# A fused attention and two-layer kernel on one core: layer two of batch 3 in seven half-size products, and a new order of all pieces

## The chip, the core and the metric

The kernel runs on one core of one Trainium2 chip. A core has five engines that run side by side and wait for each other by semaphores: TensorE (PE, matrix products; its weight loads are a row of their own, PEld), VectorE (DVE), ScalarE (ACT), GpSimd (POOL) and SyncE (SP, which issues transfers). SBUF is the core's working memory, PSUM the small memory that PE writes its products to, in banks; POOL does not read PSUM. The metric is the device time of one execution in microseconds (us), less being better; each time given is the median of a few runs.

## What is computed

The input is x (8 batches, 8 heads, 512 tokens, 64 features) and state (8, 8, 32, 64). Tokens read the state and the state reads the tokens, each with a softmax; both results go, with the heads side by side (512 features), through a layer of 2048 and back:

```python
scores = scale * np.matmul(x, state.transpose(0, 1, 3, 2))
a = softmax(scores)                      # over the 32 states
xread = np.matmul(a, state)
a2 = softmax(scores transposed)          # over the 512 tokens
sread = np.matmul(a2, x)
x = concatenate([xread, sread], axis=2)  # 544 rows a batch, heads joined: 4352 x 512
h = x @ w_in                             # 512 -> 2048
g = s * relu(h) ** 2 + b
out = g @ w_out                          # 2048 -> 512
```

Inputs and output are 32-bit floats; the kernel computes its products in 16-bit floats and adds up in 32 bits.

## The kernel before, in words

The kernel is a set of small pieces and one long list of words, ORDER (line 15). A loop at the end (line 720) walks the list and calls one function a word: the word's first part is the piece, the rest its arguments (V, A and G mean VectorE, ScalarE and GpSimd; numbers are batch, block, half). No scheduler moves anything afterwards: each engine executes its own instructions in the order in which the list issues them, and waits where a semaphore is not yet up. The order of the list is therefore the schedule.

A batch passes through these pieces:

- x.b (line 176) issues two transfers of the batch's tokens on GpSimd's queue; for batch 0, four transfers on SyncE bring 32-bit tokens (xf), which castx turns to 16 bits. xT transposes on DVE. T.b (line 290) is 16 packed products that give the scores. U, mu, D, E1, z, At and A are the token softmax: transpose, maximum, difference, exponential on ACT, sum and reciprocal, product, transpose back. keep copies the scores to SBUF.
- M.b.j (line 422) is 8 packed products, state times a quarter j of w_in, so that layer one takes the softmax weights A instead of xread; Mc copies it to SBUF. "Packed" means that several small products use parts of PE's array at once.
- l.b.f (line 474) is layer one for 128 of the 2048 hidden features: two products of 512 columns, and a relu on ACT. lh.b.f.p does two such f for half of the tokens (batch 0). s and sh square the result on the engine named, into the batch's tile g.
- nm, nms, E2, a2, aps, a2T, V and srd are the other softmax, over tokens, and the state's read; V is 32 packed products a batch.

Layer two comes in two forms. The plain form is L.b.rr.q (line 497): four products of 512 columns for 128 tokens, 16 pieces and 64 products a batch, and out.b.rr (lines 509 and 517) scales by s, adds the bias and stores. The other form splits the batch's g and w_out into 2 x 2 blocks and needs seven block products instead of eight, at the price of sums. P.b.u (line 582) is half of one block product: 8 products of 256 columns, 14 pieces and 112 products a batch. S.b.i (line 561) makes the sums of blocks of g; sum 1, 2 and 4 are written over blocks of g, sum 3 into a tile of its own, and sum 3 has to read block (1, 0) before sum 1 writes it. wsum (line 528) makes the sums T1 to T4 of w_out's blocks once. ev.b.name (line 596) takes a product out of PSUM, scaled, added to the bias or to what is there; there are seven a batch, and put (line 604) issues two stores each on SyncE. Before the change, batches 0 to 3 use the plain form and batches 4 to 7 the seven products. The state rows of all batches (lsr, ssr, S_sr, P_sr, ev_sr) go through the same two layers at the end, also with seven products.

```python
    PRODUCTS = [
        ("X", (0, 0), (0, 0)), ("Y", (0, 1), (1, 0)), ("X", (0, 0), "T2"), ("W", (1, 0), "T1"),
        ("X", None, "T3"), ("W", (0, 1), (1, 1)), ("X", (1, 1), "T4"),
    ]
```

X, Y and W are PSUM banks; X is written four times on top of itself and taken out after each, W twice.

idle.n (line 663) is n products of ones by ones that nobody reads.

Buffers set further waits. Layer one has two PSUM banks (ps_h), layer two and the idle products two (ps_o), and an argument of T and M chooses one of two double banks (ps_t, ps_a). GpSimd's transfers go round eight semaphores: the ninth is issued when the first has landed. The words win.j and wout.q load quarters of w_in (two transfers) and w_out (one), st the states of the later batches.

Of the kernel before, what the change touches and what calls it, by code (L numbers as in the profile page):

```python
# [12 lines left out]


ORDER = [
    "win.0 castx.0.0.V castx.1.0.A idle.2 idle.5 idle.9 casts.V xT.0.0.0 pair.0.4 xT.0.1.0 T.0.1.0 U.0.0 "
    "sb mu.0.0 win.1 castx.1.1.A xT.0.1.1 x.1 D.0.V.0 E1.0.0 castx.0.1.V xT.0.0.1 turn.0.4.A z.0.0 "
    "At.0.V.0 A.0.0 M.0.0.0 Mc.0.0.A keep.0.0 win.2 T.0.0.1 U.0.1 M.0.1.1 Mc.0.1.A mu.0.1 D.0.V.1 "
    "keep.0.1 E1.0.1 xT.1.0 lh.0.2.0 M.1.0.0 Mc.1.0.A lh.0.0.0 xT.1.1 T.1.1 lh.0.6.0 wout.0 z.0.1 "
    "At.0.V.1 A.0.1 lh.0.2.1 win.3 U.1 M.0.2.0 lh.0.0.1 Mc.0.2.V wout.1 sh.0.2.1.V keep.1 sh.0.0.0.G mu.1 "  # L20
    "sh.0.2.0.G lh.0.4.0 wout.2 sh.0.4.0.G D.1.V L.0.0.0 l.0.11 M.1.1.0 Mc.1.1.A L.0.1.0 l.0.8 sh.0.6.0.V "
    "l.0.9 M.0.3.0 Mc.0.3.V M.1.2.1 x.2 l.0.10 Mc.1.2.V wout.3 E1.1 z.1 lh.0.6.1 At.1.V s.0.8.2.A L.0.0.1 "
    "l.0.13 L.0.1.1 l.0.14 cps.0 cps.1 cps.2 M.1.3.1 A.1 Mc.1.3.V l.0.12 s.0.12.2.V s.0.10.2.G l.0.15 "
    "s.0.14.2.A L.0.1.2 l.1.4 l.1.7 L.0.0.2 l.1.1 l.1.2 sh.0.6.1.V st xT.2 x.3 pair.4.16 cps.3 L.0.0.3 "
# [12 lines left out]
    "l.3.0 L.2.0.1 M.4.1.1 Mc.4.1.A M.4.2.0 l.3.3 L.2.0.2 l.3.1 l.3.5 s.2.12.4.V s.3.0.4.A aps.4 xT.5 "
    "L.2.1.3 Mc.4.2.V l.3.6 l.3.8 wsum.T1.0.V L.2.0.3 L.3.0.0 l.3.14 turn.12.16.A l.3.15 T.5.1 out.2.1 "
    "l.3.4 s.3.4.2.A a2T.4.V out.2.0 L.2.2.0 L.2.2.1 L.2.2.2 L.2.2.3 nm.5 V.4 U.5 nms.5.A mu.5 D.5.G "
    "wsum.T1.1.V E2.5.1 E2.5.0 M.4.3.1 srd.4 l.3.12 out.2.2 x.6 A.4 l.3.9 xn.5 a2.5 nm.2 nms.2.V xn.2 "  # L40
    "s.3.6.2.A L.2.3.0 l.3.13 E2.2.1 Mc.4.3.A wsum.T2.2.V aps.5 a2T.5.V l.3.10 L.2.3.1 L.2.3.2 L.2.3.3 "
    "l.3.11 V.3 E1.5 l.4.2 l.4.14 L.3.2.0 L.3.2.1 srd.3 out.2.3 l.4.13 M.5.1.0 Mc.5.1.A M.5.0.1 l.4.3 "
    "Mc.5.0.A s.3.8.4.V L.3.2.2 s.3.12.4.V l.4.6 xT.6 x.7",
    "l.4.0 L.3.0.1 l.4.1 s.4.0.2.A z.5 L.3.2.3 T.6.1 U.6 M.5.2.0 E2.2.0 l.4.15 l.4.5 L.3.0.2 L.3.0.3 "
    "s.4.2.2.A wsum.T3.1.G l.4.9 nm.6 L.3.1.0 Mc.5.2.A l.4.4 L.3.1.1 out.3.2 out.3.0 l.4.12 At.5.G A.5 "
    "wsum.T3.0.G a2.2 nm.0 L.3.1.2 nms.6.A L.3.1.3 l.4.7 s.4.12.2.V s.4.14.2.V E2.6.0 aps.2 a2T.2.V "
    "out.3.1 l.4.11 L.3.3.0 E2.6.1 mu.6 l.4.8 s.4.4.4.V L.3.3.1 L.3.3.2 xT.7 l.4.10",
    "l.5.0 s.4.10.2.V V.5.2 srd.5 L.3.3.3 out.3.3 srd.2 l.5.1 M.5.3.0 M.6.0.1 s.4.8.2.V Mc.5.3.A D.6.G "
    "a2.6 E1.6 P.4.0 l.5.3 P.4.1 Mc.6.0.A ev.4.X1 l.5.7 l.5.13 P.4.2 P.4.3 M.6.2.0 S.4.3.2.V S.4.1.0.V "
    "S.4.1.1.V M.6.1.1 nms.0.A E2.0.1 S.4.2.0.V S.4.2.1.V l.5.2 Mc.6.2.A l.5.6 S.4.4.2.G ev.4.Y P.4.4 "  # L50
    "Mc.6.1.A P.4.5 z.6 l.5.4 ev.4.X2 s.5.0.2.A aps.6 a2T.6.V P.4.6 l.5.12 P.4.7 T.7.1 s.5.12.2.A keep.7 "
    "s.5.2.2.A At.6.V A.6 l.5.10 ev.4.W1 P.4.8 P.4.9 l.5.14 nm.7 wsum.T4.2.V ev.4.X3 P.4.10 P.4.11 "
    "ev.4.W2 E2.0.0 nms.7.A l.5.8 a2.0 l.5.5 s.5.4.4.V xn.6 xn.0 P.4.12 aps.0 l.5.15 s.5.14.2.G U.7 mu.7 "
    "a2T.0.A P.4.13 ev.4.X4 l.5.9 l.6.3 put.4.0.0 P.5.0 l.6.2 l.5.11 D.7.G V.6.0 s.5.8.2.V srd.6 l.6.9 "
    "l.6.8 srd.0 s.5.10.2.V E1.7 S.5.3.0.V S.5.3.1.V P.5.2 P.5.1 l.6.5 ev.5.X1 P.5.3",
    "l.6.0 l.6.1 M.6.3.0 S.5.1.2.V Mc.6.3.A xn.7 xn.1 M.7.0.1 Mc.7.0.A l.6.7 ev.5.Y P.5.6 P.5.7 z.7 "
    "S.5.2.2.V M.7.1.1 Mc.7.1.A E2.7.1 l.6.15 s.6.0.4.V l.6.14 nm.1 S.5.4.1.G P.5.4 P.5.5 ev.5.X2 ev.5.W1 "
    "l.6.10 M.7.2.1 S.5.4.0.V E2.7.0 M.7.3.0 Mc.7.3.A At.7.V P.5.8 l.6.13 l.6.4 P.5.9 a2.7 l.6.11 "
    "s.6.8.2.A s.6.4.2.G P.5.10 ev.5.X3 P.5.12 s.6.10.2.A l.6.6 A.7 l.7.2 nms.1.A E2.1.1 P.5.11 l.6.12 "
    "P.5.13 aps.7 l.7.3 ev.5.W2 Mc.7.2.V l.7.10 s.6.6.2.G E2.1.0 P.6.2 a2T.7.A l.7.6 s.6.14.2.V ev.5.X4 "  # L60
    "s.6.12.2.V S.6.3.0.V S.6.3.1.V a2.1 P.6.0 P.6.1 ev.6.X1 l.7.7 l.7.8 S.6.1.2.V put.4.0.1 S.6.2.0.V "
    "S.6.4.0.G S.6.2.1.V P.6.3 l.7.11 l.7.1 aps.1 P.6.4 P.6.5 a2T.1.A put.4.1.0 put.4.1.1 l.7.5 l.7.4 V.1",
    "l.7.0 ev.6.Y P.6.6 P.6.7 s.7.0.2.A s.7.2.2.A srd.1 ev.6.X2 P.6.8 P.6.9 l.7.14 ev.6.W1 P.6.10 l.7.9 "
    "put.5.0.0 ev.6.X3 put.5.0.1 l.7.13 V.7 srd.7 l.7.15 s.7.8.2.V s.7.10.2.V s.7.14.2.V l.7.12 P.6.12 "
    "P.6.13 ev.6.X4 s.7.12.2.V lsr.13 lsr.12 S.6.4.1.G P.6.11 ev.6.W2 lsr.7 s.7.4.4.G S.7.3.0.G lsr.14 "
    "P.7.0 P.7.1 S.7.3.1.G S.7.1.1.V lsr.4 lsr.2 P.7.2 S.7.1.0.G ssr.12.2.A ev.7.X1 S.7.2.1.V lsr.15 "
    "lsr.6 P.7.3 put.5.1.0 lsr.10 lsr.11 S.7.2.0.V ev.7.Y P.7.4 S.7.4.0.V P.7.6 P.7.5 ssr.14.2.V lsr.1 "
    "ev.7.X2 ssr.6.2.V lsr.3 P.7.7 ev.7.W1 lsr.5 ssr.4.2.V",
    "lsr.0 ssr.0.2.V P.7.8 P.7.9 ssr.2.2.V S_sr.3.0.V ev.7.X3 lsr.9 S.7.4.1.V lsr.8 P.7.10 P.7.11 "
    "ssr.8.2.A ssr.10.2.V S_sr.3.1.G put.5.1.1 put.6.0.0 S_sr.1.2.V S_sr.2.2.G S_sr.4.0.G put.6.0.1 "  # L70
    "put.6.1.0 put.6.1.1 ev.7.W2 P.7.12 put.7.0.0 put.7.0.1 P.7.13 ev.7.X4 P_sr.0 put.7.1.0 "
    "ev_sr.0.0.X.0.0 P_sr.1 ev_sr.0.0.Y.1.1 P_sr.2 P_sr.3 put.7.1.1 S_sr.4.1.G ev_sr.0.1.X.0.0 P_sr.4 "
    "ev_sr.1.1.W.0.0 P_sr.5 ev_sr.1.1.X.1.1 P_sr.6 ev_sr.0.1.W.1.1 ev_sr.1.0.X.0.1",
]


# [677 lines left out]
```

## Time and profile before

| what | us |
|---|---|
| median of 3 runs | 223.57 (223.21 to 225.01) |
| the profiled execution | 222.87 |
| its span, first to last instruction | 221.1 |
| TensorE's mean granted clock in it | 0.977 |

The profile is one execution. Its page gives the busy time of each engine, then the span in 40 slices of 5.5 us with the busy share in tenths and, as PEclk, the clock that TensorE was granted. The largest groups on PE and on the other engines (columns: line, engine, operation, output and inputs, count, then busy us and mean ns of one, then idle time of the engine just before them and what ended it):

```
L461 ACT ACTIVATE r<-hps 128x512 f16<-128x512 f32 x120 | 68.1, 600 | 23.4 <-PE hps L457 23.1
L457 PE MATMUL hps<-A,M 128*128 128x512 f16 x240 | 65.8, 380 | 0.0
L501 PE MATMUL ops<-w_out,g 128*128 128x512 f16 x256 | 62.1, 379 | 0.0
L136 PEld LDWEIGHTS <-g 128*128 128x128 f16 x384 | 37.3, 98 | 9.7 <-DVE g L571 0.8
L467 POOL TENSOR_TENSOR g<-r 128x1024 f16<-128x1024 f16 (+1 forms) x9 | 18.8, 2101 | 14.9 <-ACT r L461 14.9
L571 POOL TENSOR_TENSOR g<-g 128x1024 f16<-128x1024 f16 (+1 forms) x5 | 13.6, 2731 | 18.6 <-DVE g L571 18.6
L571 DVE TENSOR_TENSOR g<-g 128x1024 f16<-128x1024 f16 (+1 forms) x15 | 13.3, 915 | 1.2 <-POOL S L571 1.1
L511 DVE SCALAR_TENSOR_TENSOR osb<-ops,sb_bc,bias_bc 128x512 f32<-128x512 f32 x16 | 11.7, 737 | 4.3 <-PE ops L501 4.2
L600 DVE SCALAR_TENSOR_TENSOR osx<-opf_X,sb_bc,bias_bc 128x512 f32<-128x512 f32 x12 | 8.9, 741 | 7.1 <-PE opf_X L136 6.3
```

hps is layer one's PSUM tile, ops layer two's in the plain form, opf_X, opf_Y and opf_W the banks of the seven products; rows of the helper mm stand as L136. The mean of a PE row is longer than the distance between two starts, since products are pipelined. A mean that mixes forms says so.

### The profile page before, as it was taken

Reading aid. Unit: us, or ns where it says so; the run is one execution under the profiler, and the core shown is the slowest. Engines: PE = TensorE matmul, PEld = TensorE weight load, DVE = VectorE, ACT = ScalarE, POOL = GpSimd, SP = SyncE. Lnnn points to the kernel's source line nnn. Section 1 sums busy time; section 2 is a strip of 40 time slices with the busy share of each in tenths; the row PEclk is TensorE's granted clock in tenths of the full one; section 3 lists DMA queues with packets and bytes.
Section 4 is the critical chain, followed back from the end, with each engine's and each line's share of the span. In section 5 each row is a group of like instructions: output and inputs, shape, how many; then the busy total and the mean of one; then the engine's idle time right before and its main releaser. Section 6 shows DMA issues by size and latency. Waiting matters only on the chain.

```text
span 221.1 us, 4579 instructions
## 1 busy us (share of the span) xinstructions
PE 209.8 (95%) x1859; PEld 120.5 (54%) x1859; DVE 172.6 (78%) x235; ACT 152.8 (69%) x258; POOL 99.9 (45%) x100
## 2 busy tenths in 40 slices
PE   7359999999999999999999999999999999999993
PEld 2124434443444435454344567777567777888882
DVE  2698998889788995697486979999985943776952
ACT  3266985988876789788886698968888767542300
POOL 8235554175057031085850507839336089250280
PEclk9955999999999999999999999999999999999999
DMA  6999997419749620449933220896900800071065
GB/s 161 224 207 206 204 165 84 86 65 134 115 69 177 128 47 0 98 80 139 220 62 76 47 52 0 99 189 114 172 6 5 185 3 0 3 166 26 3 149 135
DMA packets 23416, 22.67 MB, mean 103 GB/s; under 512 B 4196, under 2 KB 16996, under 8 KB 23396
## 3 DMA queue, kind: packets, MB, share of 16 engines
q0 software_dynamic: 16560, 12.26, 38.8%
q1 hardware_dynamic: 6160, 9.97, 18.4%
q8 instruction: 14, 0.23, 0.4%
q10 hardware_dynamic: 676, 0.16, 0.3%
q14 instruction: 6, 0.05, 0.1%
HBM read 25.72 MB, written 8.91 MB: 157 GB/s over the span
## 4 chain that ended last, share of the span: by engine, by line
PE 87%; DMA 4%; DVE 4%; ACT 1%; SPq 1%; issue 1%; DVEq 0%
PE ops L501 25%; PE hps L457 24%; PE opf_X L136 12%; PE opf_W L136 6%; PE mps L136 4%; DMA xf<-in_x_dram 3%; PE opf_Y L136 2%; PE vps L136 2%; PE aps L136 2%; PE ops_sr_X L136 2%; PE hps_sr L457 2%; PE T_None L136 2%; PE hph L136 1%; DMA out_dram<-osx 1%; PE ops_sr_W L136 1%; SPq L608 1%
## 5 line engine op out<-in xcount | busy, mean ns | idle before, releaser
L461 ACT ACTIVATE r<-hps 128x512 f16<-128x512 f32 x120 | 68.1, 600 | 23.4 <-PE hps L457 23.1
L457 PE MATMUL hps<-A,M 128*128 128x512 f16 x240 | 65.8, 380 | 0.0
L501 PE MATMUL ops<-w_out,g 128*128 128x512 f16 x256 | 62.1, 379 | 0.0
L136 PEld LDWEIGHTS <-g 128*128 128x128 f16 x384 | 37.3, 98 | 9.7 <-DVE g L571 0.8
L501 PEld LDWEIGHTS <-g 128*128 128x128 f16 x256 | 24.6, 98 | 29.3 <-issue 0.6
L457 PEld LDWEIGHTS <-M 128*128 128x128 f16 x240 | 21.5, 98 | 23.4 <-issue 5.8
L467 POOL TENSOR_TENSOR g<-r 128x1024 f16<-128x1024 f16 (+1 forms) x9 | 18.8, 2101 | 14.9 <-ACT r L461 14.9
L151 ACT CAST M<-mps 128x1024 f16<-128x1024 f32 x23 | 23.1, 1014 | 2.5 <-PE mps L136 2.5
L467 DVE TENSOR_TENSOR g<-r 128x1024 f16<-128x1024 f16 (+1 forms) x22 | 20.5, 945 | 2.7 <-ACT r L461 2.6
L571 POOL TENSOR_TENSOR g<-g 128x1024 f16<-128x1024 f16 (+1 forms) x5 | 13.6, 2731 | 18.6 <-DVE g L571 18.6
L465 ACT ACTIVATE g<-r 128x1024 f16<-128x1024 f16 (+1 forms) x19 | 21.6, 1148 | 0.2
L191 POOL DMA_DIRECT2D xn<-in_x_dram x32 | 18.6, 596 | 2.8 <-PE vps L136 2.4
L321 POOL TENSOR_TENSOR Dm<-U,mu 128x1024 f32<-128x1024 f32 x3 | 7.0, 2343 | 20.4 <-DVE mu L317 20.3
L136 PE MATMUL opf_X<-w_T,g 128*128 128x256 f16 x128 | 15.8, 273 | 0.2 <-DVE g L571 0.2
L136 PE MATMUL mps<-w_in,stT 64*32 64x512 f16 x256 | 11.8, 410 | 3.9 <-ACT stT L151 3.3
L511 DVE SCALAR_TENSOR_TENSOR osb<-ops,sb_bc,bias_bc 128x512 f32<-128x512 f32 x16 | 11.7, 737 | 4.3 <-PE ops L501 4.2
L600 DVE SCALAR_TENSOR_TENSOR osx<-opf_X,sb_bc,bias_bc 128x512 f32<-128x512 f32 x12 | 8.9, 741 | 7.1 <-PE opf_X L136 6.3
L461 ACT ACTIVATE r_sr<-hps_sr 128x256 f16<-128x256 f32 x16 | 6.0, 384 | 11.9 <-PE hps_sr L457 8.4
L571 DVE TENSOR_TENSOR g<-g 128x1024 f16<-128x1024 f16 (+1 forms) x15 | 13.3, 915 | 1.2 <-POOL S L571 1.1
L313 DVE STREAM_TRANSPOSE U<-T_None 128x1024 f32<-128x1024 f32 x7 | 8.7, 1238 | 4.6 <-PE T_None L136 3.7
L629 POOL TENSOR_TENSOR g_sr<-g_sr 128x512 f16<-128x512 f16 (+1 forms) x4 | 6.0, 1521 | 12.6 <-ACT g_sr L465 12.5
L151 DVE CAST M<-mps 128x1024 f16<-128x1024 f32 x9 | 10.8, 1208 | 0.8 <-PE mps L136 0.8
(101 smaller groups left out, 316.8 us busy)
## 6 DMA issues: line engine op xcount, KB each, us to landing
xn<-in_x_dram POOLq DMA_DIRECT2D x32, 128.0 KB, 6.4
out_dram<-osx SPq DMA_DIRECT2D x32, 128.0 KB, 2.4
xh<-in_x_dram POOLq DMA_DIRECT2D x14, 256.0 KB, 6.0
out_dram<-osb SPq DMA_DIRECT2D x24, 128.0 KB, 3.8
w_in<-in_moe_w_in_dram POOLq DMA_DIRECT2D x8, 256.0 KB, 10.4
w_out<-in_moe_w_out_dram POOLq DMA_DIRECT2D x4, 512.0 KB, 10.0
xf<-in_x_dram SPq DMA_DIRECT2D x4, 256.0 KB, 7.8
out_dram<-osb SPq DMA_DIRECT2D x4, 256.0 KB
```

The lines of the kernel that those rows point to most:

```text
L136: return nc.tensor.matmul(out, lhsT, rhs, start=start, stop=stop, tile_position=tp, is_transpose=is_transpose, skip_group_check=skip,)
L151: (engine.copy if engine is nc.scalar else engine.tensor_copy)(out, in_)
L191: nc.gpsimd.dma_start(out=xn_t[b][32 * jh : 32 * jh + 32].rearrange("t h c d -> t h (c d)"), in_=x[b].rearrange("h (t jh c) d -> jh t h (c ...
L313: nc.vector.transpose(part(U, p), part(at[b]["T", p], p))
L457: nc.tensor.matmul(hps, lhsT, rhs, start=(i == 0), stop=(i == len(terms) - 1))
L461: nc.scalar.activation(R_t[tag, q][:, i], hps, AF.Relu)
L465: nc.scalar.activation(g, r, AF.Square)
L467: e.tensor_mul(g, r, r)
L501: nc.tensor.matmul(ops_t[tag, rr], G_t[tag][:, f, P * rr : P * rr + P], w_out_f(f), start=(f == 0), stop=(f == NKF - 1),)
L511: nc.vector.scalar_tensor_tensor(osb, ops_t.pop((tag, rr)), s_bc, bias_bc, ALU.mult, ALU.add)
L571: e.tensor_tensor(out, x, y, op)
L600: nc.vector.scalar_tensor_tensor(out, fast(b, name[0]), s_bc, out if plus else bias, ALU.mult, ALU.add)
```

## The change

Only the list ORDER differs; no function does. It does four things:

- Batch 3 goes over to the seven products: its 16 L and four out are gone, 14 P, seven ev, six S and four put are there. Since the sums of w_out are needed by then, they are made earlier, and some on another engine (T1 on GpSimd, T3 on VectorE, T4 half and half).
- The unread products of the head are 10, 8 and 4 (in three places: at the start, behind sb, and behind T.0.0.1) instead of 2, 5 and 9 (all at the start): 22 instead of 16.
- Every other piece is still there, but in a new order, and some squares and copies are on another engine.
- In GpSimd's queue of transfers the order becomes win.0, x.1, win.1, wout.0, win.2, win.3 and, behind the first two squares, wout.1, wout.2, wout.3, x.2, st; before it was win.0, win.1, x.1, win.2, wout.0, win.3, wout.1 and then, with squares between, wout.2, x.2, wout.3, st.

The head, one stretch around batch 3's products, and the end (all other lines of the list are replaced in the same way; line numbers behind the list grow by one):

```diff
 ORDER = [
-    "win.0 castx.0.0.V castx.1.0.A idle.2 idle.5 idle.9 casts.V xT.0.0.0 pair.0.4 xT.0.1.0 T.0.1.0 U.0.0 "
-    "sb mu.0.0 win.1 castx.1.1.A xT.0.1.1 x.1 D.0.V.0 E1.0.0 castx.0.1.V xT.0.0.1 turn.0.4.A z.0.0 "
-    "At.0.V.0 A.0.0 M.0.0.0 Mc.0.0.A keep.0.0 win.2 T.0.0.1 U.0.1 M.0.1.1 Mc.0.1.A mu.0.1 D.0.V.1 "
-    "keep.0.1 E1.0.1 xT.1.0 lh.0.2.0 M.1.0.0 Mc.1.0.A lh.0.0.0 xT.1.1 T.1.1 lh.0.6.0 wout.0 z.0.1 "
-    "At.0.V.1 A.0.1 lh.0.2.1 win.3 U.1 M.0.2.0 lh.0.0.1 Mc.0.2.V wout.1 sh.0.2.1.V keep.1 sh.0.0.0.G mu.1 "
-    "sh.0.2.0.G lh.0.4.0 wout.2 sh.0.4.0.G D.1.V L.0.0.0 l.0.11 M.1.1.0 Mc.1.1.A L.0.1.0 l.0.8 sh.0.6.0.V "
...
-    "l.4.0 L.3.0.1 l.4.1 s.4.0.2.A z.5 L.3.2.3 T.6.1 U.6 M.5.2.0 E2.2.0 l.4.15 l.4.5 L.3.0.2 L.3.0.3 "
...
-    "lsr.0 ssr.0.2.V P.7.8 P.7.9 ssr.2.2.V S_sr.3.0.V ev.7.X3 lsr.9 S.7.4.1.V lsr.8 P.7.10 P.7.11 "
-    "ssr.8.2.A ssr.10.2.V S_sr.3.1.G put.5.1.1 put.6.0.0 S_sr.1.2.V S_sr.2.2.G S_sr.4.0.G put.6.0.1 "
-    "put.6.1.0 put.6.1.1 ev.7.W2 P.7.12 put.7.0.0 put.7.0.1 P.7.13 ev.7.X4 P_sr.0 put.7.1.0 "
-    "ev_sr.0.0.X.0.0 P_sr.1 ev_sr.0.0.Y.1.1 P_sr.2 P_sr.3 put.7.1.1 S_sr.4.1.G ev_sr.0.1.X.0.0 P_sr.4 "
-    "ev_sr.1.1.W.0.0 P_sr.5 ev_sr.1.1.X.1.1 P_sr.6 ev_sr.0.1.W.1.1 ev_sr.1.0.X.0.1",
+    "castx.1.0.V win.0 casts.V idle.10 turn.0.4.A pair.0.4 castx.0.0.V xT.0.0.0 xT.0.1.0 T.0.1.0 U.0.0 "
+    "mu.0.0 castx.1.1.A keep.0.0 sb idle.8 D.0.V.0 xT.0.1.1 castx.0.1.V E1.0.0 x.1 z.0.0 xT.0.0.1 "
+    "At.0.V.0 M.1.0.0 Mc.1.0.A M.0.0.1 A.0.0 Mc.0.0.A win.1 T.0.0.1 U.0.1 mu.0.1 D.0.V.1 keep.0.1 idle.4 "
+    "lh.0.0.0 wout.0 lh.0.2.0 xT.1.0 M.0.1.0 xT.1.1 E1.0.1 z.0.1 T.1.1 Mc.0.1.A lh.0.4.0 win.2 win.3 "
+    "sh.0.0.0.G At.0.V.1 A.0.1 keep.1 sh.0.2.0.G sh.0.4.0.V lh.0.6.0 L.0.1.0 U.1 lh.0.4.1 lh.0.0.1 wout.1 "
+    "sh.0.6.0.V sh.0.4.1.V mu.1 D.1.V lh.0.2.1 M.0.2.1 Mc.0.2.A lh.0.6.1 sh.0.6.1.V wout.2 L.0.0.0 l.0.8 "
...
+    "L.2.3.2 l.3.14 s.3.12.4.A l.3.4 L.2.3.3 out.2.3 M.5.0.1 Mc.5.0.A V.4 srd.4 a2.5 s.3.8.4.V L.2.2.0 "
+    "At.4.G L.2.2.1 L.2.2.2 A.4 l.4.2 l.4.6 L.2.2.3 M.5.2.1 E1.5 s.3.4.4.V S.3.3.2.V S.3.1.0.G M.4.3.0",
+    "l.4.0 Mc.4.3.A xT.6 P.3.0 S.3.2.0.G l.4.1 out.2.2 l.4.3 nms.2.A z.5 P.3.1 ev.3.X1 l.4.9 E2.2.1 "
+    "S.3.1.1.V S.3.2.1.G aps.5 Mc.5.2.V E2.2.0 a2T.5.V l.4.11 a2.2 P.3.4 l.4.5 P.3.2 P.3.3 S.3.4.2.V "
...
+    "lsr.13 P.7.6 P.7.7 ssr.4.2.A ev.7.W1 P.7.8 ssr.6.2.V S.7.4.0.V S_sr.1.0.V lsr.10 lsr.15 P.7.9 lsr.11 "
+    "P.7.10 ev.7.X3 lsr.14 ssr.14.2.V lsr.12 ssr.12.2.V ssr.10.2.V S_sr.3.1.V S_sr.2.0.V S_sr.3.0.G "
+    "S_sr.1.1.V S_sr.2.1.V P.7.11 ev.7.W2 P.7.12 P.7.13 P_sr.0 P_sr.1 ev_sr.0.0.X.0.0 put.7.0.0 ev.7.X4 "
+    "ev_sr.0.0.Y.1.1 P_sr.2 ev_sr.0.1.X.0.0 S_sr.4.2.V put.7.0.1 put.7.1.0 put.7.1.1 P_sr.3 P_sr.4 "
+    "ev_sr.1.1.W.0.0 P_sr.5 ev_sr.1.1.X.1.1 ev_sr.0.1.W.1.1 P_sr.6 ev_sr.1.0.X.0.1",
 ]
```

90 rows, old and new, of the table ORDER are left out of this document.

## The prediction, made before the changed kernel was run

> **What bounds the kernel now.** I read the page's busy shares and slices, then the chain of waits, then the head in windows, then the timeline where the chain leaves TensorE.
>
> ```profile
> PE 209.8 (95%) x1859; PEld 120.5 (54%) x1859; DVE 172.6 (78%) x235; ACT 152.8 (69%) x258; POOL 99.9 (45%) x100
> PE   7359999999999999999999999999999999999993
> PEclk9955999999999999999999999999999999999999
> ```
>
> TensorE (PE) is full from slice 5 (22 us) to the end; only the head has gaps, and there the granted clock is half. A busy PE need not be at its pace, so the chain of waits (start, length, what) is read for the pace:
>
> ```profile
> 44.88 1.73 PE ops L501 x8
> 46.61 0.86 PE hps L457 x4
> 47.47 0.56 PE mps L136 x16
> 48.02 0.54 PE hps L457 x2
> ...
> 139.66 1.75 PE opf_X L136 x16
> ```
>
> A 512-column product takes 1.73/8 = 216 ns, a 256-column one of the half-size kind 1.75/16 = 109 ns. These are full streams: adding such pieces up from the start of L.0.0.0 (22.28) gives 193.9 us, and the last product ends 195.05 us after it. So PE waits almost nowhere, and the time is: arrival at the full stream, plus PE's work, plus 3.8 us behind the last product.
>
> The packed pieces (M, T, V, cps, which use parts of the array) carry a toll. Two M's stand as 0.56, one alone elsewhere as 0.34: 0.22 each and 0.12 for the visit; the two products behind take 0.54 where 0.43 is usual. So a visit costs 0.21 to 0.23 beyond its work.
>
> The head, in the 3.41 us windows in which the clock changes (columns: length, busy of PE, its loads, DVE, ACT, POOL, clock, DMA share, GB/s):
>
> ```profile
> 7.67:11.08 3.41, 0.46 (x4) 0.29 (x3) 2.26 (x6) 1.15 (x3) 0.75 (x1) 1.00 1.21 217
> 11.08:14.49 3.41, 1.70 (x32) 0.48 (x32) 3.02 (x6) 2.02 (x4) 1.97 (x3) 0.50 1.16 208
> 14.49:17.90 3.41, 2.75 (x32) 1.24 (x32) 3.34 (x6) 3.09 (x5) 0.00 (x0) 0.50 1.24 205
> 17.90:21.32 3.42, 3.31 (x32) 0.99 (x16) 2.95 (x5) 1.89 (x4) 2.41 (x3) 0.50 1.25 210
> 21.32:24.73 3.41, 3.41 (x34) 1.77 (x27) 3.15 (x4) 2.83 (x6) 0.93 (x2) 1.00 1.23 203
> ```
>
> PE does almost nothing in one window and then has half its clock for three.
>
> **The change, part by part.** It is reckoned against the profiled execution: 222.87 us with a span of 221.1, 0.70 below the median of 223.57. I carry the difference over to the median.
>
> *Products.* Batch 3 loses 16 L pieces (64 products) and gets 14 P pieces (112): 16 x 0.864 = 13.82 against 14 x 0.873 = 12.23, so -1.6. The weight loads grow by 48 of 98 ns, and lie beside: 8 x 98 = 784 ns under 873. The Trainium skill (TensorE: Matmul & The Clock Gate, Back-to-back issue gap) speaks against the exchange: it gives 131 ns a product in a stream at 512 columns and 81 at 128. Halving between them by columns, an estimate from that page is 98 at 256, and 112 x 98 - 64 x 131 would be +2.6. This trace disagrees, with 216 and 109.
>
> *Order.* PE enters packed work 32 times before and 27 times after: 5 x 0.21 = -1.05.
>
> *Other engines.* Per instruction, by the mean row of its kind: DVE gets 7 evictions for 4 (0.74 each: +2.2) and batch 3's sums S3, half of S1, S4 (1.20 + 0.69 + 1.20); POOL gets three halves (2.12 each). The weight sums change hands: T1 goes from DVE (2 x 0.68) to POOL (2 x 2.15), T3 from POOL (2 x 2.15) to DVE (1.22), half of T4 to POOL. Over the whole list DVE has +3.3, POOL +4.0, ACT +1.1, on 48, 121 and 68 us of idle time. I cost them at nothing, but the cover is thin at batch 3. Behind L.2.3.3, DVE must do out.2.3, a2.5, s.3.8.4 and A.4 (0.66 + 0.75 + 1.14 + 0.63 between starts, 0.2 to begin: 3.4), and l.4.2 needs A.4 after 3.55 of PE work. From there s.3.4.4, S3 (1.14 + 1.13) and POOL's S1 and S2 halves (2.12 each) with their hand-overs take 6.7, and P.3.4 needs them after 6.74. What is late there stalls PE in full. I add 0.3 for such places (0 to 2).
>
> *Head.* POOL's DMA queue gets x.1 ahead of win.1, wout.0 ahead of win.2, and wout.1 to wout.3 in one train behind two squares. Transfers land one by one, 1.25 us for a w_in or x half (12.05, 13.31, 14.49, 15.86 in this trace) and 2.5 for a w_out quarter. In the new order win.0 is here at 11.09, x.1 at 13.3, win.1 at 15.9, wout.0 at 18.4, win.2 at 20.9, win.3 at 23.4, then the other quarters at 25.9, 28.4 and 30.9. Steps, at the full clock: ACT holds E1.0.0 until the cast of xf (8.99), the copy of T and two small ones are done, so it runs 10.2 to 10.8 (before 10.71); z, xT, At, A follow on DVE, A.0.0 ends at 13.4 (before 13.82). M.1.0.0 and M.0.0.1 wait for win.0 alone and their copies end at 13.5 on ACT; T.0.0.1 runs at 12.7, idle.4 covers to 14.05, lh.0.0.0 and lh.0.2.0 end at 14.95. M.0.1.0 waits for win.1 (15.95), its copy ends at 17.3, T.1.1 fits in between. lh.0.4.0 and lh.0.6.0 run from 17.4, L.0.1.0 at 18.4 with wout.0. U.0.1, mu, D, both xT.1, z and At bring A.0.1 at 18.7 (before 19.82), so lh.0.4.1 starts at 19.25. The next two wait for ACT to empty their banks, M.0.2.1 for win.2 (21.05), and l.0.8 for ACT's copy of it: 22.75. By then PE has behind it what it had before at 22.28, and two lh (0.87) and two L (1.73): 2.6 us more work for 0.47 more time, so -2.1. Later quarters land 0.5 to 1 us ahead of their use.
>
> This stands on the clock. idle.8 puts 1.7 us of products, and sb 0.4, in the window where 0.46 were, and idle.4 0.9 in the next. Where the level lies this trace does not show: 0.46 of 3.41 lost the clock, 2.98 (4.26 to 7.67) kept it. 2.1 is nearer to the latter. The Trainium skill (TensorE: Matmul & The Clock Gate, Part 1: The HAM clock gate) wants a window of about 3.4 us idle before it halves the clock; the longest gap left here would be 1.3 us, and by that rule the clock holds.
>
> *Tail.* SyncE's stores, before:
>
> ```profile
> 210.29 3.75 SPq L608 DMA_DIRECT2D out_dram<-osx  x6
> 214.13 0.55 SPq L706 DMA_DIRECT2D out_dram<-osr  x1
> 214.73 1.25 SPq L608 DMA_DIRECT2D out_dram<-osx  x2
> 216.13 2.29 SPq L706 DMA_DIRECT2D out_dram<-osr  x3
> ```
>
> Twelve issues of 0.55 to 0.63; they begin 0.76 us before P_sr.0 starts (211.05), and the last (217.88) just follows the last eviction. In the new order ev.7.W2, which frees them, stands on DVE behind ssr.12, ssr.10 and four sums. lsr.12 ends 2.6 before P_sr.0, its relu 0.6 later; six instructions of 0.35 and the eviction (0.75) make 0.9 after P_sr.0. The twelve need 7.4 from 1.0, and the last starts at 7.85, where before it was 6.83: +1.0 (0 if DVE is early, 1.5 with hand-overs).
>
> *Sum.* -1.6 - 1.05 - 2.1 + 1.0 + 0.3 = -3.45: span 217.7, on the median 220.1.
>
> **Rivals.** *The clock halves anyway.* For it: 1.70 and 2.75 busy of 3.41 did not bring the clock back. Idle.4 then takes 1.7, each lh 0.97, and l.0.8 comes at 25.0 instead of 22.75: 222.4, no change that can be told.
>
> *DVE and POOL collide.* A DVE tensor-tensor that meets a POOL one is held:
>
> ```profile
> 192.20 2.12 POOL L571 TENSOR_TENSOR S<-g 128x1024 f16<-128x1024 f16 x1 [4.24 <-DVE g L467]
> 194.27 2.12 POOL L571 TENSOR_TENSOR g<-g 128x1024 f16<-128x1024 f16 x1
> 194.35 2.59 DVE L571 TENSOR_TENSOR g<-g 128x1024 f16<-128x1024 f16 x1 [1.09 <-POOL S L571]
> ...
> 199.69 1.05 PE L136 MATMUL opf_X<-w_T,g 128*128 128x256 f16 x8 [0.23 <-DVE g L571]
> 200.21 0.68 DVE L571 TENSOR_TENSOR g<-g 128x1024 f16<-128x1024 f16 x1
> ```
>
> 2.59 instead of 0.68 is +1.9, and PE's only stall in the stream (0.4) follows. The new order puts POOL halves beside DVE sums for batch 3 (S.3.1.1 against S.3.2.0 and S.3.2.1), 5 (S.5.1 against S.5.2.1) and 7 (S.7.1.0 against S.7.3.1), with covers of 0.1 to 1.3 us. All three uncovered give 5.7: 225.8, slower. One gives 222.0, two 223.9; it decides from three. Against it: five such collisions before cost PE 0.4 in all.
>
> *Half-size products fall behind their loads.* At 123 ns each (13.82/112) the gain is gone; 98 ns of load under 109 leaves 11 ns. That would be 221.7, the same as before. All 56 P pieces here kept 0.87 except where packed work followed (0.97). By the estimate from the Trainium skill's page above (Back-to-back issue gap) it would be +2.6 for -1.6, 224.3.
>
> That batch 3 does not take the new path is no rival: the new list has P.3.0 to P.3.13, its evictions and stores, and no L.3 or out.3.
>
> **How the numbers follow.** The forecast has 0.52 (own range 218.8, with no stall and no loss in the tail, to 222.0, with one collision uncovered): 0.49 of it faster, 0.03 the same. The clock has 0.22, the same. The collisions have 0.18: 0.16 for three or more, slower, 0.02 for two, the same. The loads have 0.02, the same. A head that waits 1 to 2 us for a transfer that lands late has 0.06 (221.1 to 222.1), half faster, half the same. About 1%, 2.2 us, is what a measurement of this kernel can tell from no change, so 221.3 to 225.8 counts as the same. Faster 0.49 + 0.03 = 0.52; same 0.03 + 0.22 + 0.02 + 0.02 + 0.03 = 0.32; slower 0.16. The range reaches over the clock to two collisions with a stall more: 218.8 to 224.8; outside lie the 0.16 and a little below.
>
> **What would show it.** PEclk without the two 5s; l.0.8 near 22.8; P.3 pieces of 0.87 back to back; 27 visits to packed work; the last out_dram<-osr issue gated by SP itself and not by DVE; DVE tensor-tensors of 2 us and a PE wait on "DVE g" if the collisions count. A half clock after 11 us, or PE waits above 2 us in the stream, would make it wrong.

## The result, and the profile after

The changed kernel takes 228.27 us (227.43 to 230.60, four runs), where the kernel before took 223.39 (222.76 to 225.01) beside it: a ratio of 1.0255, 95% interval 1.0202 to 1.0308. It is slower by 2.6%. The forecast of 220.1 was 8.2 us too low, and the range, which ended at 224.8, did not hold the time. The profiled execution took 229.09 us with a span of 227.3, 6.2 more than the 221.1 of before.

First the page, the rows that answer to those shown of before:

```profile
PE 211.4 (93%) x1913; PEld 127.2 (56%) x1913; DVE 173.8 (76%) x239; ACT 153.0 (67%) x260; POOL 103.3 (45%) x99
PE   7687999938999999999999999999999999999990
PEclk9969999995999999999999999999999999999997
```

The head is denser than before in slices 2 and 3, as forecast, and its clock drops in one slice only. New are a 3 in slice 9 (45 to 51 us) and a half clock in slice 10 (51 to 57 us), in the middle of a stream that was full before. One hole: everything behind it is full to the end. Three rows of the view of waits name it (engine, line and what it wanted, what it waited for, us in total, times, longest):

```profile
DVE xT L289 <- DMA xh<-in_x_dram: 5.0, 1, 5.0
PE T_None L137 <- DVE xT L289: 4.6, 1, 4.6
PE mps L137 <- DMA w_in<-in_moe_w_in_dram: 1.3, 1, 1.3
```

The third row is the head. The first two are one chain: TensorE waits 4.6 us for DVE's transpose of batch 3's tokens (xT.3), and DVE waits 5.0 us for the load that brings them (x.3). The timeline around it, TensorE and then GpSimd (start, length, engine, line, operation, tiles, and in brackets the idle time before and what ended it):

```profile
45.01 1.89 PE L502 MATMUL ops<-w_out,g 128*128 128x512 f16 x8
46.83 0.41 PE L137 MATMUL mps<-w_in,stT 64*32 64x512 f16 x8
51.80 1.05 PE L137 MATMUL T_None<-xT,stE 32*32 32x512 f16 x16 [4.56 <-DVE xT L289]
52.79 1.89 PE L458 MATMUL hps<-A,M 128*128 128x512 f16 x4
54.47 3.42 PE L502 MATMUL ops<-w_out,g 128*128 128x512 f16 x8
```

```profile
38.41 1.89 POOL L468 TENSOR_TENSOR g<-r 128x1024 f16<-128x1024 f16 x1 [14.38 <-ACT r L462]
40.24 0.17 POOL L180 COPY ahead<-xT 1x2 f16<-1x2 f16 x1
40.36 1.14 POOL L183 DMA_DIRECT2D xh<-in_x_dram  x2
```

The new order has x.3 behind the square s.1.2.2.G on GpSimd. That square waits 14.38 us for ScalarE, and so the load is issued at 40.36, 4.3 us later than before (36.03). The same eight products take 1.89 us ahead of the hole and 3.42 behind it. The windows of 3.4 us there say why (columns as in the prediction: length, busy of PE, its loads, DVE, ACT, POOL, clock, DMA share, GB/s):

```profile
47.30:50.70 3.40, 0.00 (x0) 0.00 (x0) 0.20 (x1) 0.55 (x1) 0.00 (x0) 1.00 0.27 81
50.70:54.10 3.40, 2.30 (x20) 0.64 (x21) 3.37 (x4) 0.00 (x0) 0.72 (x1) 0.50 0.22 82
54.10:57.50 3.40, 3.40 (x10) 1.19 (x9) 1.33 (x2) 1.08 (x2) 2.39 (x4) 0.50 0.21 27
57.50:60.90 3.40, 3.40 (x17) 1.57 (x16) 2.66 (x4) 2.54 (x7) 0.00 (x0) 0.99 0.81 139
```

One window with TensorE empty, and the next two run at half clock. The Trainium skill (TensorE: Matmul & The Clock Gate, Part 1: The HAM clock gate) states this rule, an idle window of about 3.4 us halves the clock; this trace agrees, with 0.00 us of products in 3.40. From 48.0 to 50.4 no engine computes at all: this hole is a wait for one transfer.

The transfer itself was slow. DMA activity from 38 to 52 us, in 40 slices of 0.35, and the rows of the issues (last number: median us from issue to landing):

```profile
DMA  0000001412012169679999964222222222222222
...
out_dram<-osb SPq DMA_DIRECT2D x3, 256.0 KB
xh<-in_x_dram POOLq DMA_DIRECT2D x2, 256.0 KB, 8.7
```

Before, the same two halves of x.3 took 4.0. Here the DMA engines are full only from 43 to 46.5 us; after that they are two tenths busy, and x.3 is still not there until 50.4. Stores of batch 0, issued at 39.01, 40.80 and 45.55, are what else is under way.

The accounts of the two profiled executions, by the starts of l.0.8 and the end of the last product (before: the point with equal work behind TensorE, as in the prediction, 24.88):

| | before | after | difference | forecast |
|---|---|---|---|---|
| head, to that point | 24.88 | 24.15 | -0.73 | -2.1 |
| from there to the last product's end, without the hole | 192.45 | 190.35 | -2.10 | -2.35 |
| the hole: wait 4.63, half clock 2.75 | 0 | 7.38 | +7.38 | 0 |
| last product's end to the span's end | 3.77 | 5.42 | +1.65 | +1.0 |
| span | 221.1 | 227.3 | +6.2 | -3.45 |

The 4.63 is the start of T.3.1 less that of M.2.0.0, less the 0.34 that such a piece takes; the 2.75 is what T.3.1, l.1.13, l.1.14, L.0.3.2 and L.0.3.3 take (5.93, from 51.80 to 57.73) beyond the 3.18 that they take where the clock is full (46.64 to 49.82 in the first run below).

### The profile page after: what moved, and what is told of

Read it like the earlier page. It is cut to its first block, busy times and chain, and to the rows that moved or that the text cites. A ratio compares the mean times of both kernels' runs of the same rounds, so it can differ in the third digit from the quotient of the medians.

```text
span 227.3 us, 4695 instructions
## 1 busy us (share of the span) xinstructions
PE 211.4 (93%) x1913; PEld 127.2 (56%) x1913; DVE 173.8 (76%) x239; ACT 153.0 (67%) x260; POOL 103.3 (45%) x99
## 4 chain that ended last, share of the span: by engine, by line
PE 83%; DMA 8%; ACT 3%; POOL 1%; DVE 1%; issue 1%; DVEq 0%; POOLq 0%
PE hps L458 22%; PE ops L502 16%; PE opf_X L137 15%; PE opf_W L137 8%; DMA xh<-in_x_dram 4%; DMA w_in<-in_moe_w_in_dram 4%; PE opf_Y L137 4%; PE mps L137 3%; PE hps_sr L458 3%; PE vps L137 2%; PE hph L137 2%; PE aps L137 2%; PE ops_sr_X L137 2%; PE T_None L137 1%; ACT M L152 1%; POOL g L468 1%
## 5 line engine op out<-in xcount | busy, mean ns | idle before, releaser
L137 PEld LDWEIGHTS <-g 128*128 128x128 f16 x480 | 46.7, 98 | 11.1 <-issue 0.4
L502 PE MATMUL ops<-w_out,g 128*128 128x512 f16 x192 | 48.7, 389 | 0.0
L502 PEld LDWEIGHTS <-g 128*128 128x128 f16 x192 | 19.0, 100 | 23.0 <-issue 2.8
L572 POOL TENSOR_TENSOR g<-g 128x1024 f16<-128x1024 f16 (+1 forms) x6 | 16.0, 2662 | 13.9 <-DVE S L572 9.3
L137 PE MATMUL opf_X<-w_T,g 128*128 128x256 f16 x160 | 19.6, 273 | 0.0
L468 DVE TENSOR_TENSOR g<-r 128x2048 f16<-128x2048 f16 (+1 forms) x18 | 17.9, 1005 | 1.2 <-ACT r L462 1.2
L343 POOL TENSOR_TENSOR At<-E,rz 128x1024 f16<-128x1024 f16 x4 | 8.0, 1989 | 19.9 <-DVE rz L334 11.9
L601 DVE SCALAR_TENSOR_TENSOR osx<-opf_X,sb_bc,bias_bc 128x512 f32<-128x512 f32 x15 | 11.2, 747 | 6.6 <-PE opf_X L137 4.7
L289 DVE STREAM_TRANSPOSE xT<-xh 128x1024 f32<-128x1024 f32 (+2 forms) x12 | 10.3, 870 | 5.8 <-DMA xh<-in_x_dram 5.0
L512 DVE SCALAR_TENSOR_TENSOR osb<-ops,sb_bc,bias_bc 128x512 f32<-128x512 f32 x12 | 8.9, 738 | 6.7 <-PE ops L502 6.7
L152 DVE CAST M<-mps 128x1024 f16<-128x1024 f32 x9 | 10.9, 1210 | 0.7 <-PE mps L137 0.5
L333 DVE TENSOR_REDUCE z<-E 128x32 f32<-128x1024 f16 (+1 forms) x9 | 9.8, 1088 | 2.1 <-ACT E L328 2.1
```

The costliest lines, as they stand in the source:

```text
L137: return nc.tensor.matmul(out, lhsT, rhs, start=start, stop=stop, tile_position=tp, is_transpose=is_transpose, skip_group_check=skip,)
L152: (engine.copy if engine is nc.scalar else engine.tensor_copy)(out, in_)
L289: nc.vector.transpose(part(out, p, g), part(in_, p, g))
L333: nc.vector.tensor_reduce(part(z, p), blk(part(at[b]["E1"], p)), AX.X, ALU.add)
L468: e.tensor_mul(g, r, r)
L502: nc.tensor.matmul(ops_t[tag, rr], G_t[tag][:, f, P * rr : P * rr + P], w_out_f(f), start=(f == 0), stop=(f == NKF - 1),)
```

## The experiments

Theory A: the loss is the load x.3, late by its issue and slow by the stores beside it, and the half clock that the wait brings. Rival B: the half-size products of batch 3, or collisions of DVE and GpSimd (two of their instructions holding each other up), cost the time. All medians stand against runs of the kernel before on the same chip; runs on different chips are compared by these ratios.

**x.3 one place earlier.**

```diff
-out.0.2 s.1.2.2.G x.3 Mc.2.1.A
+out.0.2 x.3 s.1.2.2.G Mc.2.1.A
```

> The changed kernel with the load of batch 3 (x.3) one place earlier on GpSimd, ahead of the square s.1.2.2.G. Theory A (the whole loss is this load: in the changed kernel it is issued at 40.4, behind a square that waits for ScalarE, and lands at 50.4; TensorE waits 4.6 us for it and then runs at half clock for about 3): it is issued near 37.0 and lands by 42, T.3.1 starts without a wait, and the time is 228.3 - 7.5 = about 220.8, between 219.5 and 222. Rival B (the half-size products of batch 3, or DVE and POOL tensor-tensors that collide, cost the time): no change, 227 to 228.5. Rival C (only the wait counts, the clock halves anyway in this stretch): about 223.7.

Measured 221.46 us (before 223.13; ratio 0.9941, 0.9909 to 0.9973). Two words exchanged take away 6.8 us, and the changed kernel is then 0.6% faster than before. The load is issued at 36.71. TensorE's timeline at the same place, and the issue row of the load:

```profile
44.48 1.89 PE L502 MATMUL ops<-w_out,g 128*128 128x512 f16 x8
46.30 0.41 PE L137 MATMUL mps<-w_in,stT 64*32 64x512 f16 x8
46.64 0.64 PE L137 MATMUL T_None<-xT,stE 32*32 32x512 f16 x16
```

```profile
xh<-in_x_dram POOLq DMA_DIRECT2D x2, 256.0 KB, 4.0
```

T.3.1 follows its neighbour without a gap, and the load takes 4.0 again. Theory A holds; B, as the cause of the loss, falls. This profiled execution (222.57) has another, smaller wait, 1.15 us at 131 us; it comes up again below.

**x.3 late in the kernel before.** The opposite edit, one word moved in the old order:

```diff
-xT.2 x.3 pair.4.16
+xT.2 pair.4.16
...
-sh.0.4.1.G L.0.2.0
+sh.0.4.1.G x.3 L.0.2.0
```

> The kernel before, with x.3 alone moved behind the square sh.0.4.1.G on GpSimd, so that it is issued at 40.1 in place of 36.0, between the same two stores. Theory A: it lands near 50 in place of 40.95, DVE's xT.3 (44.62 before) starts 5 to 6 us later and what stands behind it on DVE (z.2, At.2, the copy of M.2.0) makes TensorE wait 3 to 5 us, perhaps with a half clock: 226 to 231. Rival (the place of this load does not matter in an order that is otherwise that of before): 223 to 224.

Measured 229.51 (ratio 1.0283, 1.0215 to 1.0351). The old order loses as much by this one word as the new order did. Its issue row, its longest wait for a load, and TensorE:

```profile
xh<-in_x_dram POOLq DMA_DIRECT2D x2, 256.0 KB, 9.1
```

```profile
DVE xT L288 <- DMA xh<-in_x_dram: 6.3, 2, 6.1
```

```profile
55.49 1.06 PE L136 MATMUL mps<-w_in,stT 64*32 64x512 f16 x16 [4.17 <-DVE M L151]
56.48 3.59 PE L501 MATMUL ops<-w_out,g 128*128 128x512 f16 x8
```

Here TensorE does not wait for xT.3 itself but for a copy of M that stands behind it in DVE's queue.

**The stores later, x.3 untouched.** The first two stores of batch 0 are kept back and issued behind the third:

```diff
-out.0.0 T.2.1
+out.0.0.late T.2.1
...
-keep.2 out.0.1 mu.2
+keep.2 out.0.1.late mu.2
...
-out.0.2 s.1.2.2.G
+out.0.2 owed s.1.2.2.G
```

> The changed kernel with x.3 where it is (issued near 40.4), but the first two stores of batch 0 (out.0.0, out.0.1) issued on SyncE behind the third, at about 45.6 instead of 39.0 and 40.8. Theory A1 (the load takes 7.9 and 9.4 us instead of 3.6 and 4.4 because it shares the DMA engines with these stores): it lands at 44 and 45, xT.3 ends by 47 and the wait of 4.6 us is gone or below 0.5; the time is near 221. Rival A2 (the load is late by its issue alone, and slow whatever else runs): it lands near 50 again, 227.5 to 228.5.

Measured 225.07 (ratio 1.0110, 1.0058 to 1.0162): the wait at T.3.1 is gone, but the time is not near 221. x.3 was issued at 39.5, some 0.9 us sooner than in the changed kernel and 3.5 later than before, but alone. DMA activity and issue rows from 36 to 48 us:

```profile
DMA  0000000000000000989999999600000011505032
...
out_dram<-osb SPq DMA_DIRECT2D x3, 256.0 KB
xh<-in_x_dram POOLq DMA_DIRECT2D x2, 256.0 KB, 3.9
```

It took 3.9 and the hole at 47 is gone. So the 8.7 came from the stores, not from the late issue. But the three stores now go out together at 44.7 to 46.0, the next load x.4 (49.4) meets them, takes 9.4, and DVE waits 5.4 us for it; behind that, TensorE's timeline has a wait of 2.89:

```profile
65.27 1.02 PE L502 MATMUL ops<-w_out,g 128*128 128x512 f16 x4 [2.89 <-DVE osb L518]
```

The expectation overlooked this, as the prediction had overlooked x.3.

**The stores in four parts, no word moved.** A store of batch 0 is one DMA whose outermost dimension is j = 4. Here each j is a DMA of its own, with 32 rows:

```diff
-            store(b, rr, [rows.rearrange("(t r j) n -> r j t n", r=SCH, j=4)[rr]])
+            store(b, rr, rows.rearrange("(t r j) n -> r j t n", r=SCH, j=4)[rr], 4)
```

> The changed kernel, its order untouched, with each store of batch 0 issued as four DMAs of 64 KB (one for each j) in place of one of 256 KB whose outermost dimension is j = 4. In the trace a store of batch 0 moves about 25 packets of 2 KB in 0.5 us at 0.08 us each, as if on four of the sixteen engines, where the stores of the later batches (outermost dimension 32) move 50 to 64. Theory A1': the load x.3 is slow because a quarter of its packets stand on those four engines behind the stores; with the stores spread over all sixteen they are done soon, x.3 (issued at 40.4) lands by 45.5, TensorE's wait of 4.6 us falls below 1 us and the time is 220.5 to 222.5. Rival A2': stores and loads share a total rate; the spread changes nothing and x.3 lands near 49 to 50: 227 to 228.5.

Measured 222.35 (before 222.46; ratio 0.9998, 0.9977 to 1.0019). Without any change of the order the time is 5.9 us less in the medians, and by the ratios (1.0255 and 0.9998) the whole loss is gone. DMA activity and issue rows from 36 to 48 us, then TensorE at T.3.1:

```profile
DMA  0000000000457458968989899999983293753810
...
out_dram<-osb SPq DMA_DIRECT2D x12, 64.0 KB, 1.7
xh<-in_x_dram POOLq DMA_DIRECT2D x2, 256.0 KB, 5.0
```

```profile
47.39 0.64 PE L137 MATMUL T_None<-xT,stE 32*32 32x512 f16 x16 [0.88 <-DVE xT L289]
```

The stores no longer leave a long row of twos, the load, issued at 39.6 with stores beside it (0.7 us sooner than in the changed kernel, 3.6 later than before), takes 5.0, and 0.88 of the wait is left. The Trainium skill (DMA: Bandwidth & Descriptors, Rules for kernel authors) says that an outermost dimension smaller than 16 confines a DMA to at most that many of the 16 engines. Two tenths busy while such stores run alone fits four of sixteen; which engines they were, the profile doesn't show.

**Unread products in the wait.** Twenty products of 512 columns ahead of T.3.1, into the bank that T.3.1 uses next; nothing reads them:

```diff
-T.3.1 nm.3 l.1.13
+hold.20 T.3.1 nm.3 l.1.13
```

> The changed kernel with twenty unread 512-column products (20 x 0.216 = 4.3 us) on TensorE ahead of T.3.1, where it waits for x.3. They take the place of the wait and add no work that anything reads. Theory A: the load still lands near 50.4 and T.3.1 still starts near 51.8, but the granted clock stays at full behind it, so the pieces T.3.1 to L.0.3.3 take their usual 3.1 us instead of 5.9: 2.8 us less than the profiled run of the changed kernel, about 226 (225.2 to 226.5). If the half clock cost nothing: 228.

Measured 227.05 (ratio 1.0170, 1.0130 to 1.0210), 1.2 below the changed kernel in the medians and 2.0 in the profiled executions. The load still lands at 50.4 and T.3.1 starts at 51.79, but the clock stays:

```profile
50.50:53.00 2.50, 2.08 (x24) 0.65 (x22) 2.47 (x3) 0.00 (x0) 0.00 (x0) 1.00 0.23 88
53.00:57.00 4.00, 4.00 (x20) 1.85 (x19) 3.86 (x5) 2.49 (x6) 3.11 (x4) 1.00 0.10 20
```

T.3.1 to L.0.3.3 take 3.18 here (51.79 to 54.97) in place of 5.93, so in the trace the half clock is a cost of its own, on top of the wait. In the medians its size is smaller and not clear of noise: the two intervals just overlap (1.0202 to 1.0308 against 1.0130 to 1.0210). The mean clocks of the changed kernel's four runs are 0.972, 0.965, 0.985 and 0.985, so the two shorter ones spent less time at half clock; where in the run, these figures do not say.

**Batch 3 in whole products.** With x.3 early, layer two of batch 3 as before: L.3 and out.3 in the places of P.3 and ev.3, the sums S.3 and the stores put.3 left out of the order.

> The kernel with x.3 early, but layer two of batch 3 in sixteen pieces of 512-column products (L.3 with four evictions) as before, in the places of the fourteen half-size ones; the sums S.3 on DVE and GpSimd are gone too. The prediction's term: 16 x 0.864 - 14 x 0.873 = 1.6 us more, about 223.0. Rival B (the half-size form of batch 3 gives back what it saves in sums, evictions and waits): 221.5 or less.

Measured 222.87 (before 222.46; ratio 1.0019, 0.9994 to 1.0044) against 0.9941 with the half-size products: 0.0078 of 223, 1.7 us, from runs on two chips. The prediction's term was 1.6. The intervals do not meet; together they leave about 1 us to either side.

**No sums on GpSimd in batch 3.** With x.3 early, S.3.1.0, S.3.2.0 and S.3.2.1 on DVE.

> The kernel with x.3 early, with the three halves of batch 3's sums that GpSimd does (S.3.1.0, S.3.2.0, S.3.2.1) on DVE instead, so that none of its tensor-tensors meets a GpSimd one there. The prediction's rival (collisions of DVE and GpSimd cost up to 1.9 us each): 0.5 to 2 us faster than 221.5. Theory (no wait of TensorE stands there, so the collisions were hidden): 221.5, within 0.5; up to 1 us slower if the three sums on DVE (1.2 to 1.4 each in place of 2.1 beside it) make P.3.4 late.

Measured 222.01 (ratio 0.9985, 0.9958 to 1.0012), not faster than with the collisions (0.9941). DVE, now with three sums more, lets TensorE wait once:

```profile
106.67 1.03 PE L137 MATMUL opf_X<-w_T,g 128*128 128x256 f16 x8 [0.48 <-DVE osx L601]
```

**No unread products in the head.** With x.3 early, without idle.8 and idle.4.

> The kernel with x.3 early, without idle.8 and idle.4, the unread products in the head behind the first ten. The prediction's theory (they hold the clock in the head): the clock halves from about 11 to 20 us as it did before, and l.0.8 comes 1 to 2 us later than 23.6: 222.5 to 223.5. Rival (the head is set by the landing of w_in and w_out and by ScalarE's copies, so the clock of TensorE matters little there): l.0.8 moves by less than 0.6, 221.3 to 222.

Measured 222.66 (ratio 0.9999, 0.9971 to 1.0027) against 0.9941: 1.3 us slower by the ratios, from runs on two chips. The clock does what the prediction said:

```profile
PEclk9857999999999999999999999999999999999997
```

But l.0.8 starts at 23.89 in this trace and at 23.63 with the products and no half clock at all: 0.26. What the unread products are worth lies between; neither theory gave both numbers.

**The tail.** With x.3 early, ev.7.W2 ahead of the sums of the last group, the stores of batch 7 right behind their evictions:

```diff
-S_sr.3.1.V S_sr.2.0.V S_sr.3.0.G S_sr.1.1.V S_sr.2.1.V P.7.11 ev.7.W2 P.7.12 P.7.13
+P.7.11 ev.7.W2 put.7.0.0 put.7.0.1 S_sr.3.1.V S_sr.2.0.V S_sr.3.0.G S_sr.1.1.V S_sr.2.1.V P.7.12 P.7.13 ev.7.X4 put.7.1.0 put.7.1.1
```

> The kernel with x.3 early, and in the tail ev.7.W2 ahead of four sums on DVE, with the stores of batch 7 moved up to their evictions. In the changed kernel the last store is issued 1.7 us after the last eviction has begun, behind SyncE's own queue; before it just followed the eviction. Theory (SyncE's queue sets the end): its eight stores start 1.5 to 2 us earlier, the last one is issued right behind the last eviction, and the span after TensorE's end is 4.0 instead of 5.45: 1.3 less than the kernel with x.3 early, about 220.1. Rival (the sums that are now behind ev.7.W2 hold up P_sr.2, which reads S2): TensorE waits 0.3 to 1 at P_sr.2 and the gain is 0.3 to 1.

Measured 220.58 (ratio 0.9921, 0.9882 to 0.9960). SyncE's last issues, first those of the changed kernel (last product's end 221.88), then these (214.25):

```profile
216.64 1.19 SPq L609 DMA_DIRECT2D out_dram<-osx  x2
218.24 0.55 SPq L707 DMA_DIRECT2D out_dram<-osr  x1
218.84 3.82 SPq L609 DMA_DIRECT2D out_dram<-osx  x6
222.76 1.85 SPq L707 DMA_DIRECT2D out_dram<-osr  x3
```

```profile
207.18 6.03 SPq L609 DMA_DIRECT2D out_dram<-osx  x8
213.31 2.51 SPq L707 DMA_DIRECT2D out_dram<-osr  x4
```

The issues now begin 7.1 us before the last product's end, where they began 5.2 before it, and the span ends 4.35 behind it in place of 5.42. In the ratios the gain over the kernel with x.3 early is 0.2% (0.4 us), inside the intervals, so the 1.3 of the theory is not shown. P_sr.2 is held by 0.24 only.

**The kernel before with its stores in four.**

> The kernel before, with the stores of batch 0 in four DMAs each, nothing else. Its x.4 was issued at 49.2, beside a store, and took 7.0 and 8.8 us, and its xn.3 11 to 12 us, but TensorE waited for neither. Theory: they land 2 to 4 us sooner and the time stays within 0.3% of before (222.3 to 223.5), since in that order every load has more slack than the stores cost. Rival (shared engines cost it time as well): 1 us or more faster.

Measured 222.89 (before 222.26; ratio 1.0011, 0.9983 to 1.0040). The loads from 48 to 62 us land much sooner, x.4 in 4.4 us (7.9 before), xn.3 in 6.7 (10.9), and nothing gains by it: in that order no load was waited for.

**All mends together.** x.3 early, the tail, the stores in four, and put.7.1 issued from ScalarE's queue.

> All mends together: x.3 early, the tail of e6_tail, the stores of batch 0 in four DMAs, and the last four stores of batch 7 issued from ScalarE's queue, which is idle by then, so that SyncE has four fewer in front of the last ones. Theory: the last store is issued right behind the last eviction (0.5 us sooner than in e6_tail, where SyncE needs 2.5 us for the last four), and later loads (x.4) no longer share four engines with the stores, which nothing waited for here: 219.8 to 220.4, ratio to before about 0.988. If SyncE's queue was not the end, it is 220.6 as e6_tail.

Measured 220.08 (before 222.26; ratio 0.9913, 0.9887 to 0.9940). It beats the kernel before by 0.9% and, by the ratios, the changed kernel by some 3.3%. Over the tail alone nothing can be told (0.9921). Its profiled execution, the longest of eleven (221.95), shows the wait at 131 us again:

```profile
DVE osx L601 <- DMA out_dram<-osx: 4.3, 2, 2.9
PE opf_X L137 <- DVE osx L601: 1.5, 1, 1.5
```

**xn.0 behind the sum S.4.4.2.** The same kernel with these four loads later:

```diff
-S.4.1.2.V xn.0 l.5.9
+S.4.1.2.V l.5.9
...
-S.4.4.2.G P.4.4
+S.4.4.2.G xn.0 P.4.4
```

> The kernel with all mends, and the four loads of xn.0 moved on GpSimd behind the sum S.4.4.2 (from 126.4 to about 135; V.6.0 reads them at 149.8). In the profile of the kernel with all mends, eight xn loads are issued at 124.0 to 128.6 beside eight stores of batch 3; the store that frees the first output tile takes 6.7 us in place of 2.4, DVE's next eviction into that tile waits for it, and TensorE waits 1.7 us (opf_X). Theory (the same sharing of DMA engines, from the other side): with four loads fewer the store lands 1 to 3 us sooner, TensorE's wait falls from 1.7 to below 0.8, the time is 219.0 to 219.8, ratio to before 0.985 to 0.989. Rival (the wait is of this one profile and not in the median): 220.1 as the kernel with all mends.

Measured 220.21 (five runs; before 222.66; ratio 0.9890, 0.9855 to 0.9926). The store that frees the tile lands in 4.2 us instead of 6.7, and TensorE's wait is gone from the profile. The median is that of the kernel above, as the rival said; the wait is likely absent from most runs, but only one execution of each was profiled.

## Why the prediction was wrong

**The step that failed** is "Other engines", with its "I cost them at nothing" and its 0.3 for thin places. It counted the instructions that DVE, GpSimd and ScalarE gain, and looked for thin cover at batch 3's sums only. It left out a DMA that the new order moves: x.3 goes behind s.1.2.2.G on GpSimd's queue, a square that waits for ScalarE, and into the company of the stores out.0.0 and out.0.1. The slack was there to be read: before, x.3 landed at 40.95 and DVE took it up at 44.62. In the new order it landed 9.4 later, at 50.4: 4.3 by the late issue and 5.1 by the slow transfer (its second half took 9.4 from issue to landing instead of 4.4). By its late issue alone it would have landed near 45.3 and, behind the eviction that keeps DVE until 45.5, been transposed by 46.8, just ahead of T.3.1's turn at 47.2. The runs with the stores later (no wait there) and in four parts (0.88) bear this out, though the load was issued 0.9 and 0.7 sooner in them. What the prediction did count was no larger than it said: DVE is busy 1.2 us longer than before, GpSimd 3.4 and ScalarE 0.2, and no wait of TensorE stands at the instructions that it named.

The rows that would have warned were in the trace of before. Its x.4, issued at 49.2 beside a store of batch 0, took 7.0 and 8.8 us. The prediction did have a rival with a transfer that lands late, but only in the head, for 1 to 2 us.

**The clock.** The rival "the clock halves anyway" meant the head. The half clock that cost most came in another place, where the new wait emptied a whole window. In the head of the changed kernel's profile it lasted one window and not three, and with x.3 early it was absent. But the prediction's step that the clock holds there because no gap is long enough failed in that profile: the longest gap was 1.30 us, as forecast, and the clock fell all the same, behind a window with 1.19 us of products (last section).

**Products, -1.6.** Right, as far as the intervals tell: 1.7 by the run with whole products. The half-size products kept 109 ns (1.75 us for 16) to the end of the trace, and did not fall behind their loads.

**Order, -1.05, and the thin places, +0.3.** With the products they make -2.35; the trace has -2.10 without the hole. l.4.2, P.3.4 and P.3.8 started without a wait. No run takes the two terms apart.

**Collisions.** They did not count: no wait of TensorE stands at them, and taking batch 3's away gave nothing. The 0.16 that the prediction gave to "slower" rested on them; slower came from elsewhere.

**Head, -2.1.** Mis-sized: -0.73 in the profile. It went as reckoned up to T.0.0.1 (12.72); then idle.4 and the two lh behind it ran at half clock, and lh.0.4.0, which waited 1.19 for ScalarE's copy of M, started at 18.71 and not at 17.4. With the full clock and x.3 early it started at 17.68 and l.0.8 at 23.63 in place of 24.15, so about 0.5 of the missing 1.4 is the clock. The rest is landings reckoned too early, in that run M.0.1.0's w_in (16.14, not 15.95) and above all L.0.1.0's w_out (19.23, not 18.4).

**Tail, +1.0.** Right in kind (SyncE's queue starts late behind ev.7.W2), +1.65 in size. The prediction started the stores 1.0 us after P_sr.0, and they did (216.64 against 215.61); but the last issue came 8.4 after it and not 7.85.

So the hole explains the sign, and not all of the miss: without it, with x.3 early, the change is worth 0.6%, 1.3 us, where the forecast was 3.45. In that run's profile, against the forecast, the head takes 0.85 more, the tail 0.7 more, and the wait at 131 us is 1.15.

## What to carry to other kernels

When an order moves a load, find its issue in the queue of the engine that issues it, what that engine waits for ahead of it, and which other transfers it will share the DMA engines with; a landing time from an undisturbed place is not its price elsewhere. The stores with an outermost dimension of 4 held up the loads beside them; splitting them cost nothing that can be measured here, took off 5.9 us where a load had no slack, and nothing where it had. A wait of TensorE can cost more than itself: behind waits of 4.2 and 4.6 us the clock was half for 6.8 us, behind one of 2.9 it stayed full.

## What the runs showed of the hardware

Stores of 256 KB with an outermost dimension of 4 kept the DMA engines two tenths busy and stretched a 256 KB load beside them from 4.0 us to 9.1 (median of its two halves) beside two stores, in the kernel before with x.3 late, and to 8.7 in the changed kernel, where a third followed; with the stores issued later another load, beside them, took 9.4. Eight loads of 128 KB beside a store of 128 KB stretched that from 2.4 to 6.7, and four to 4.2.

By the granted clock in narrow windows, the changed kernel's clock changed at 13.18, 16.60, 50.73, 57.56 and 224.81 us, all whole multiples of 3.413 apart. With x.3 early it changed once, at 218.73, behind the last product; counted back from there, windows of that run begin at 10.51 and 13.93. In the head the clock fell behind a window with 1.19 us of products, and held behind ones with 2.51 and 2.48, in runs with the same order there. First the changed kernel, then the one with x.3 early:

```profile
9.80:13.20 3.40, 1.19 (x33) 0.48 (x32) 3.00 (x6) 1.56 (x3) 1.78 (x3) 1.00 1.16 205
13.20:16.60 3.40, 3.40 (x20) 1.59 (x18) 3.31 (x5) 1.57 (x3) 0.14 (x1) 0.50 1.24 206
```

```profile
10.51:13.93 3.42, 2.51 (x40) 0.99 (x39) 3.19 (x8) 1.95 (x3) 1.40 (x3) 1.00 1.18 204
13.93:17.34 3.41, 2.48 (x33) 1.08 (x31) 3.34 (x6) 2.90 (x5) 2.12 (x3) 1.00 1.25 207
```

An empty window is not needed. Nor does the busy time alone decide: counted in the same way, the clock fell behind windows with 1.76 (the stores later) and 1.97 (x.3 late in the kernel before) and held behind one with 1.73 (batch 3 in whole products). Whether the packed products of that stretch count for less stays open.
